# Memory-augmented attention mixed with a GEGLU: products of the memory from float16 pairs instead of float32

## The chip, the cores and the metric

The kernel runs on one core of a Trainium2 chip, as one launch. The metric is the device time of that launch in microseconds (us). Before the change it is 1577.5 us, the median of three runs (1577.44 to 1577.76). The inputs and the output are float32 in DRAM.

## What is computed

The input has 2048 tokens of D = 576 features. Its output is a mix, by a gate per token, of a segmented attention with a memory and of a feed-forward block with GELU gating:

```python
# attention, 32 heads of 18, four segments of 512 tokens
for s in range(4):
    qs, ks, vs = q[:, :, s], k[:, :, s], v[:, :, s]
    p = softmax(qs @ ks.T * 18**-0.5 + mask)         # within the segment
    a_dot = p @ vs
    pq = phi(qs)                                     # phi(t) = t + 1 if t > 0 else exp(t)
    a_mem = (pq @ M) / (pq @ z + 1e-6)
    o = g * a_mem + (1 - g) * a_dot                  # g = sigmoid(beta) per head
    pk = phi(ks)
    M = M + pk.T @ vs                                # 18 x 18 per head
    z = z + pk.sum(tokens)
a = concat(o) @ wo
b = (gelu(x @ w_gate) * (x @ w_up)) @ w_down         # 4608 hidden features
gate = sigmoid((x * gate_w).sum(-1))
out = gate * a + (1 - gate) * b
```

What the change touches is the line of M and the line of z. For each segment but the last, all heads' M and z are products over the segment's 512 tokens.

## The kernel before

**Float16 pairs.** For TensorE (PE) the kernel splits most operands into a high half (the value rounded to float16) and a low half (what is left, rounded to float16), and forms three products: high by high, high by low and low by high. The products of the memory are an exception: they are float32.

**The parts of the kernel.** The first part makes keys, queries and values, and the memory; it ends near 219 us of the profiled span. Then come 72 feed-forward steps (`step`, L1132), which hold the attention of all heads between their own products, and at the end the output projection. The change is in the first part, except that attention later reads the stored value pairs.

**The first part** has four stages s, one for each segment of 512 tokens. A stage first works on tokens in four quarters q of 128, and then on columns in nine groups j of 128 (queries and keys together have nine such groups). Stage 0 does its rows in a way of its own at the start (L623 to L684). From stage 1 on, with p = s - 1, the loop at L795 to L837 issues in each quarter:

- `vrows(s, q, 0)` (L518): the values of this quarter's tokens, heads 0 to 15, as fourteen float16 products of 288 columns into a PSUM bank.
- `put_rows` (L493): ScalarE (ACT) writes the high half of the value pairs to `vstage`, and for s up to 2 a float32 copy of the values to `v32`, whose last column in each head GpSimd (POOL) has set to 1. VectorE (DVE) writes the low half later (`rest`, L510), and then a DMA stores the pairs to DRAM for the attention.
- `key_rows(p, q - 1)` (L566): six float32 transposes of the previous segment's phi of keys (features by tokens, 128 x 512 tiles) to tokens by features; four go to a bank of the tag `st`, two to the bank `V`. ScalarE copies both to the tile `krow` in two pieces, of 448 and 192 columns.
- `beside_rows`, `behind_rows` (L706, L727): work of VectorE, ScalarE and GpSimd for the later feed-forward part, put here by quarter and stage. `form_sums` (L352) is the one that the prediction speaks of: in stages 2 and 3 it holds VectorE for more than a microsecond at a time.
- `recall(p, q)` (L534), from stage 2 on: phi of the queries of segment p times the memory as it stands, five float32 products into two banks of `st`; `put_recall` (L544) then divides by the z column on VectorE, which reads those banks until its end.
- `vrows(s, q, 1)` and `put_rows`: the same for heads 16 to 31 and two more columns (one is the mix's gate).
- `memorize(p, q - 1)` (L578): for each of the five spans of 128 features one float32 product, `krow` (as the stationary operand) by `v32` of the heads that the span touches, summed over the quarters in the banks `U` (spans 0 to 2) and `pv` (spans 3 and 4). A span touches 8 heads of 18 + 1 = 19 columns, so 152 columns; the last one, of 64 features, touches 4 heads, 76 columns. What a span has beside the heads' own blocks is masked away later.

Quarter 3's `key_rows` stands behind the loop over quarters, and its `memorize` behind the first column group.

Then, for each j, `project(s, j)` (L460) issues fourteen float16 products of 512 columns, and `put_columns` (L467), one group later, takes them out of PSUM: ScalarE writes the high half of queries and keys to `stage`, and the exponential part of phi; VectorE writes the linear part of phi (L480), its sum with the other (L481, or GpSimd) and the low half (`words`, L486), and a DMA stores the pairs. At j = 1, `keep_memory(p)` (L588) multiplies the products by the mask `bdm` and adds them to the block-diagonal memory `bd`, which the next recalls read. `make_gate` (L601) also stands there, and `beside_products` (L738) places side work by j.

**What sets the order.** For PE, ACT, DVE and POOL the order of the instructions on each engine is the order in which the program issues them (`manual_schedule(engines=ORDERED)`, L608). DVE's halves of `put_rows`, `put_columns` and `recall` are not issued where they are written: they are appended to the list `later`, and `finish_later` (L456) issues all of it, at two places in a quarter and one in a column group. The DMA queue (SP) is ordered by the framework. The pieces of one engine's queue are strictly in order, so an instruction that waits holds all behind it.

**Banks.** The program has eight PSUM banks of 512 float32 columns, given out by tag: `G`, `U`, `V` and `pv` have one each, `st` and `dn` two each, used in turn. A product into a bank waits until the bank's last reader is done. `project` uses `G` for j = 0, 4 and 8, `U` for 3 and 7, and `st` for the others.

## Time and profile before

One execution was profiled; that execution's span and engine totals are these:

| what | before |
|---|---|
| median of three runs | 1577.5 us |
| span of the profiled execution | 1576.7 us |
| instructions | 32594 |
| TensorE busy (matmul) | 1571.1 us, 100% |
| TensorE busy (weight loads, beside the matmuls) | 936.6 us, 59% |
| VectorE busy | 1134.6 us, 72% |
| ScalarE busy | 1175.1 us, 75% |
| GpSimd busy | 1209.5 us, 77% |
| DMA | 209.87 MB, 133 GB/s in the mean |

How to read what follows. Lines such as L585 are lines of the kernel before. PE is TensorE's matmul, PEld its weight load (the stationary operand), which runs beside the matmul ahead of it; DVE is VectorE, ACT ScalarE, POOL GpSimd. A timeline row gives the start, the length, the engine, the line, the operation, and output and input by the program's names with their shapes; "x12" joins twelve records that follow each other, and what stands in brackets is idle time ahead of it with what ended it. Matmul records of neighbours overlap, so that TensorE's pace is read from one start to the next, and a few matmul records are missing from a trace. The "chain that ended last" is followed back from the last instruction, at each step to what released it; its shares say which engine's work made up the span.

### The profile page before, as it was taken

The page shows a single profiled execution, that of the slowest core. Times are in us where ns is not written, and L with a number is a line of the kernel's source. Part 1 is how long each engine was busy: PE and PEld are TensorE (multiplying, and loading weights), DVE is VectorE, ACT ScalarE, POOL GpSimd, SP SyncE. Part 2 cuts the span into 40 slices and gives each one's busy share as a digit, 9 for nine tenths or more (in the row PEclk, how much of TensorE's full clock was granted, in tenths as well). Part 3 has the DMA queues.
Part 4 walks back from the last instruction along what each step waited for, and adds up shares of the span by engine and source line. Part 5 has one row for each costly group of instructions (what it writes and reads, how often), then busy time and mean ns, then how long its engine had stood idle before and what let it go on. Part 6 is the DMA issues. An engine that isn't in the chain of part 4 may idle for free.

```text
span 1576.7 us, 32594 instructions
## 1 busy us (share of the span) xinstructions
PE 1571.1 (100%) x11864; PEld 936.6 (59%) x11864; DVE 1134.6 (72%) x2974; ACT 1175.1 (75%) x1996; POOL 1209.5 (77%) x1173
## 2 busy tenths in 40 slices
PE   9999999999999999999999999999999999999999
PEld 6666754555555555555555555555555555555577
DVE  6667784777777777777777777777777777776665
ACT  6666454888888888888888888888888888886421
POOL 2233756788888888898988888887879797788697
PEclk9999999999999999999999999999999999999999
DMA  6532442587878798879787899888897887774644
GB/s 239 203 121 90 138 139 76 104 130 128 132 130 141 126 140 137 138 124 141 129 133 130 137 129 142 133 132 149 134 139 130 141 130 138 130 128 89 136 101 140
DMA packets 472680, 209.87 MB, mean 133 GB/s; under 512 B 427672, under 2 KB 437400, under 8 KB 472008
## 3 DMA queue, kind: packets, MB, share of 16 engines
q1 hardware_dynamic: 472520, 207.80, 71.3%
q8 instruction: 93, 1.52, 0.4%
q14 instruction: 67, 0.55, 0.1%
HBM read 91.87 MB, written 27.26 MB: 76 GB/s over the span
## 4 chain that ended last, share of the span: by engine, by line
PE 97%; DMA 1%; DVE 1%; ACT 1%; issue 0%; SPq 0%; DVEq 0%; ACTq 0%
PE dn L1007 27%; PE U L1047 18%; PE V L1047 12%; PE G L1047 12%; PE pv L962 4%; PE st L322 2%; PE U L1054 2%; PE G L322 2%; PE dn L332 2%; PE V L1059 1%; PE G L1059 1%; PE st L915 1%; PE U L322 1%; PE st L1367 1%; PE V L1054 1%; PE G L1054 1%
## 5 line engine op out<-in xcount | busy, mean ns | idle before, releaser
L942 POOL TENSOR_TENSOR ph<-pf,ph 128x512 f16<-128x512 f32 (+1 forms) x256 | 353.7, 1403 | 173.2 <-ACT ph L941 173.2
L1007 PE MATMUL dn<-paird,hh 128*128 128x288 f16 x3396 | 476.4, 286 | 0.0
L1047 PEld LDWEIGHTS <-pairg 128*128 128x128 f16 x3024 | 285.4, 98 | 304.4 <-issue 18.3
L1007 PEld LDWEIGHTS <-hh 128*128 128x128 f16 x3456 | 332.1, 98 | 153.4 <-issue 18.0
L1015 DVE SCALAR_TENSOR_TENSOR acc<-dn,ev,acc 128x288 f32<-128x288 f32 x534 | 274.3, 515 | 54.1 <-PE dn L1007 43.9
L931 ACT ACTIVATE pf<-pf,mb,esc 128x512 f32<-128x512 f32 (+3 forms) x512 | 292.9, 642 | 7.0 <-POOL ph L942 0.4
L1047 PE MATMUL G<-x,pairg 128*128 128x512 f16 x864 | 209.9, 379 | 0.2 <-DVE gl L1029 0.2
L1047 PE MATMUL U<-xt,pairg 128*128 128x512 f16 x864 | 210.0, 379 | 0.0
L1034 POOL TENSOR_TENSOR hh<-gl,hh 128x512 f16<-128x512 f32 x144 | 164.4, 1162 | 18.4 <-ACT hh L1033 18.4
L303 POOL TENSOR_TENSOR pairg<-raw,pairg 128x640 f16<-128x640 f32 (+2 forms) x144 | 174.2, 1232 | 5.1 <-ACT pairg L299 5.1
L299 ACT ACTIVATE pairg<-raw 128x640 f16<-128x640 f32 (+2 forms) x144 | 89.9, 650 | 112.9 <-POOL raw L293 65.1
L941 ACT ACTIVATE ph<-pf 128x512 f16<-128x512 f32 (+1 forms) x256 | 172.4, 720 | 0.0
L1192 DVE COPY gl<-U 128x512 f32<-128x512 f32 x72 | 49.8, 692 | 167.1 <-POOL hh L1034 150.1
L918 DVE CUSTOM_DVE_ANT_0 pf<-st,mask 128x512 f32<-128x512 f32 (+1 forms) x256 | 157.1, 614 | 0.0
L268 POOL TENSOR_SCALAR raw<-raw,sc 128x640 f32<-128x640 f32 x72 | 135.8, 1900 | 0.0
L918 DVE CUSTOM_DVE_ANT_0 pf<-dn,mask 128x256 f32<-128x256 f32 (+1 forms) x192 | 67.1, 375 | 81.6 <-PE dn L915 81.2
L1037 ACT ACTIVATE gl<-gl,sc 128x512 f32<-128x512 f32 x144 | 96.6, 715 | 37.1 <-DVE gl L1218 19.3
L1047 PE MATMUL V<-xt,pairg 128*128 128x512 f16 x432 | 105.7, 381 | 0.0
L1047 PE MATMUL U<-x,pairg 128*128 128x512 f16 x432 | 105.0, 379 | 0.0
L1047 PE MATMUL V<-x,pairg 128*128 128x512 f16 x432 | 104.8, 378 | 0.0
L1033 ACT ACTIVATE hh<-gl 128x512 f16<-128x512 f32 x144 | 82.6, 616 | 16.6 <-DVE gl L1029 16.5
L962 PEld LDWEIGHTS <-pt 128*128 128x128 f16 x2560 | 83.4, 96 | 6.3
(305 smaller groups left out, 2641.1 us busy)
## 6 DMA issues: line engine op xcount, KB each, us to landing
raw<-in_wgu_dram SPq DMA_DIRECT2D x36, 640.0 KB
rawd<-in_wd_dram SPq DMA_DIRECT2D x36, 288.0 KB
qt<-qk SPq DMA_DIRECT2D x132, 72.0 KB
kt<-qk SPq DMA_DIRECT2D x132, 72.0 KB
qk<-stage SPq DMA_DIRECT2D x36, 256.0 KB
qt<-qk SPq DMA_DIRECT2D x132, 36.0 KB
kt<-qk SPq DMA_DIRECT2D x132, 36.0 KB
vp<-vstage SPq DMA_DIRECT2D x16, 296.0 KB
```

Source lines behind the costliest of these rows:

```text
L268: pool.tensor_scalar(r, r, scl[f // 2][0][:, 0:1], None, OP.mult)
L303: pool.tensor_tensor(spot(f, *p, 1), raw_g[f][:, p[0] : p[1]], spot(f, *p, 0), OP.subtract)
L918: dve.tensor_tensor_reduce(prob[a][:, COL[qi] : COL[qi + 1]], out[qi], mask[:, L - (qi + 1) * P :], 1.0, -3e38, OP.add, OP.max, mx[a][:, q ...
L931: act.activation(r, r, AF.Exp, bias=b[:, qi : qi + 1], scale=esc[:, 0, c : c + 1])
L941: act.activation(h[:, 0, cols], p[:, cols], AF.Copy)
L942: pool.tensor_tensor(h[:, 1, cols], p[:, cols], h[:, 0, cols], OP.subtract)
L962: pe.matmul(ov, pr[:, 10 * i + COL[qi] // P + kb], v[:, 4 * e + kb, c0 : c0 + VC], start=kb == 0 and i == 0, stop=kb == qi and i == 1)
L1007: pe.matmul(o[:, :NH], hh[:, a, q * P : (q + 1) * P], w[:, b, n * NH : (n + 1) * NH], start=i == 0, stop=i == 5)
L1015: dve.scalar_tensor_tensor(av, o[:, :NH], ev, av, OP.mult, OP.add)
L1034: pool.tensor_tensor(hh[:, 1], t, hh[:, 0], OP.subtract)
L1037: act.activation(t, o, AF.Gelu_apprx_tanh, scale=scl[f // 2][0][:, 2 + c : 3 + c])
L1047: pe.matmul(o, w[:, i, (a + k) * P : (a + k + 1) * P], x[:, b + k], start=start and k == 0 and i == 0 and b == h, stop=k == 1 and i == 1, ...
```

## The change

The products of the memory are made of float16 pairs, in `memorize`, as three products for each span: high keys by high values with the ones column (19 columns a head), high keys by low values (18), and low keys by high values with the ones column (19). All three are summed in the same bank.

- **Values.** The float32 copy `v32` and its memset are gone. `memorize` reads the pairs that are stored for the attention anyway, `vstage`, straight from SBUF. For this, a head's 37 columns are stored as [low, high, 1] instead of [high, low, 1], so that the high half and the 1 lie side by side. A product's moving operand then has runs of 18 or 19 elements, 37 apart. `vstage` gets six buffers instead of four.
- **Keys.** `krow` is now a pair of float16 tiles. ScalarE writes the high half as it takes the transposed keys out of PSUM, times a power of two; VectorE writes the low half from the same PSUM banks (`low`, two instructions, appended to `later`).
- **Scales.** The pairs need the keys within float16's range. `key_scale(p)` works out the power of two in four one-column instructions on VectorE, in quarter 0 of the next stage, and `memory_scale(p)` in three more, ahead of `project(s, 0)`, the factors that undo it. `keep_memory` first scales the z columns (two instructions more) and applies the other factor with the mask in one instruction (`scalar_tensor_tensor` for `tensor_tensor`).
- **Banks.** From stage 1 on, the first four transposes of the keys go to `G` instead of `st`, and `project(s, 0)` to `dn` instead of `G`.
- **Order.** `recall(p, q)` now stands behind the second `vrows` of its quarter instead of ahead of it, and so directly ahead of `memorize`. `memorize(p, 3)` is preceded by a `finish_later()`.

```diff
--- before.py
+++ after.py
@@ -393,2 +393,3 @@
     esc = cst.tile([P, 2, 4], F32, name="esc")
+    kmc = cst.tile([P, 3, 4], F32, name="kmc")
     gha = cst.tile([P, 4, H], F32, name="gha")
@@ -409,3 +410,3 @@
         pa = first.enter_context(tc.tile_pool(name="early", bufs=2, reuse_waits="tile"))
-        W, phi, vst, v32, kr, mem = {}, {}, {}, {}, {}, {}
+        W, phi, vst, kr, mem = {}, {}, {}, {}, {}
         QG = ((0, 1), (2, 3), (4, 5), (6, 7), (8,))
@@ -427,3 +428,3 @@
             if on_act:
-                junk = pa.tile([P, KT * P], F32, name="krow", bufs=2).bitcast(BF16)
+                junk = flat(pa.tile([P, 2, KT * P], F16, name="krow", bufs=2)).bitcast(BF16)
                 act.activation(junk[:, : r.shape[1]], r, AF.Square, accum_out=o)
@@ -462,3 +463,3 @@
             i = j % 4
-            pr = bank("G") if i == 0 else bank("U") if i == 3 else bank("st", 2)
+            pr = bank("dn", 2) if s and j == 0 else bank("G") if i == 0 else bank("U") if i == 3 else bank("st", 2)
             chain_w(pr, lambda k, a: w[:, a, k * P : (k + 1) * P], x16[s])
@@ -497,7 +498,4 @@
             if b == 0:
-                st = vst[s, q] = pa.tile([P, H, VC], F16, name="vstage", bufs=4)
+                st = vst[s, q] = pa.tile([P, H, VC], F16, name="vstage", bufs=6)
                 pool.memset(st[:, :, VC - 1 : VC], 1.0)
-                if s <= 2:
-                    v32[s, q] = pa.tile([P, H, MC], F32, name="v32", bufs=6)
-                    pool.memset(v32[s, q][:, :, DH:], 1.0)
             st = vst[s, q]
@@ -505,8 +503,6 @@
             hs = slice(16 * b, 16 * b + 16)
-            act.activation(st[:, hs, 0:DH], p3, AF.Copy, scale=unit)
-            if s <= 2:
-                act.activation(v32[s, q][:, hs, 0:DH], p3, AF.Copy, scale=a)
+            act.activation(st[:, hs, DH : 2 * DH], p3, AF.Copy, scale=unit)

             def rest():
-                dve.scalar_tensor_tensor(st[:, hs, DH : 2 * DH], p3, unit, st[:, hs, 0:DH], OP.mult, OP.subtract)
+                dve.scalar_tensor_tensor(st[:, hs, 0:DH], p3, unit, st[:, hs, DH : 2 * DH], OP.mult, OP.subtract)
                 if b:
@@ -566,3 +562,3 @@
         def key_rows(s, q):
-            ka, kb = bank("st", 2), bank("V")
+            ka, kb = bank("G") if s else bank("st", 2), bank("V")
             tok = slice(q * P, (q + 1) * P)
@@ -573,5 +569,12 @@
                 pe.transpose(kb[:, i * P : (i + 1) * P], phi[s, j][:, tok], ident)
-            k = kr[s, q] = pa.tile([P, KT * P], F32, name="krow", bufs=2)
-            act.activation(k[:, :448], ka[:, 64:], AF.Copy)
-            act.activation(k[:, 448:], kb[:, :192], AF.Copy)
+            k = kr[s, q] = pa.tile([P, 2, KT * P], F16, name="krow", bufs=2)
+            sc = kmc[:, s, 1:2]
+            for o, r in ((slice(0, 448), ka[:, 64:]), (slice(448, KT * P), kb[:, :192])):
+                act.activation(k[:, 0, o], r, AF.Copy, scale=sc)
+
+            def low():
+                for o, r in ((slice(0, 448), ka[:, 64:]), (slice(448, KT * P), kb[:, :192])):
+                    dve.scalar_tensor_tensor(k[:, 1, o], r, sc, k[:, 0, o], OP.mult, OP.subtract)
+
+            later.append(low)

@@ -580,3 +583,3 @@
                 mem[s] = bank("U"), bank("pv")
-            k, v = kr.pop((s, q)), v32.pop((s, q))
+            k, v = kr.pop((s, q)), vst.pop((s, q))
             for j, (a, w) in enumerate(SPANS):
@@ -584,4 +587,7 @@
                 o = mem[s][j // 3][:, (j % 3) * 8 * MC : (j % 3) * 8 * MC + (h1 - h0) * MC]
-                pe.matmul(o, k[:, a : a + P], v[:, h0:h1].rearrange("p h d -> p (h d)"),
-                          start=q == 0 and j % 3 == 0, stop=q == 3 and j in (2, 4), skip_group_check=True)
+                o = o.rearrange("p (h d) -> p h d", d=MC)
+                for i, c in ((0, slice(DH, VC)), (0, slice(0, DH)), (1, slice(DH, VC))):
+                    pe.matmul(o[:, :, : c.stop - c.start], k[:, i, a : a + P], v[:, h0:h1, c],
+                              start=q == 0 and j % 3 == 0 and i == 0 and c.start == DH,
+                              stop=q == 3 and j in (2, 4) and i == 1, skip_group_check=True)

@@ -590,2 +596,6 @@
             n = 8 * MC
+            sm, zf = kmc[:, s, 2:3], kmc[:, s, 3:4]
+            for o, h in ((ka, 24), (kb, 12)):
+                z = o[:, : h * MC].rearrange("p (h d) -> p h d", d=MC)[:, :, DH:]
+                dve.tensor_scalar(z, z, zf, None, OP.mult)
             for o, d, k in ((ka[:, : 3 * n], flat(bd[:, 0:3]), flat(bdm[:, 0:3])),
@@ -594,7 +604,20 @@
                 if s == 0:
-                    dve.tensor_tensor(d, o, k, OP.mult)
+                    dve.scalar_tensor_tensor(d, o, sm[: o.shape[0]], k, OP.mult, OP.mult)
                 else:
-                    m = pa.tile([P, KT * P], F32, name="krow", bufs=2)[: o.shape[0], : o.shape[1]]
-                    dve.tensor_tensor(m, o, k, OP.mult)
+                    m = flat(pa.tile([P, 2, KT * P], F16, name="krow", bufs=2)).bitcast(F32)[: o.shape[0], : o.shape[1]]
+                    dve.scalar_tensor_tensor(m, o, sm[: o.shape[0]], k, OP.mult, OP.mult)
                     dve.tensor_tensor(d, d, m, OP.add)
+
+        def key_scale(s):
+            fl, iv, sm, zf = (kmc[:, s, i : i + 1] for i in range(4))
+            dve.tensor_scalar(sm, al[:, s, 0:1], 2.0**30, 1.0, OP.mult, OP.add)
+            dve.tensor_scalar(fl.bitcast(I32), sm.bitcast(I32), EXP, None, OP.bitwise_and)
+            dve.tensor_scalar(iv.bitcast(I32), fl.bitcast(I32), EXP, None, OP.bitwise_xor)
+            dve.tensor_scalar(iv, iv, 2.0**13, None, OP.mult)
+
+        def memory_scale(s):
+            fl, iv, sm, zf = (kmc[:, s, i : i + 1] for i in range(4))
+            dve.tensor_scalar(sm, fl, al[:, s, 1:2], None, OP.mult)
+            dve.tensor_scalar(zf.bitcast(I32), al[:, s, 1:2].bitcast(I32), EXP, None, OP.bitwise_xor)
+            dve.tensor_scalar(zf, zf, 2.0**-15, None, OP.mult)

@@ -805,2 +828,4 @@
                             key_rows(p, q - 1)
+                        else:
+                            key_scale(p)
                         beside_rows(s, q)
@@ -810,6 +835,6 @@
                         behind_rows(s, q)
+                        pv = vrows(s, q, 1)
+                        put_rows(s, q, 1, *pv)
                         if p >= 1:
                             recall(p, q)
-                        pv = vrows(s, q, 1)
-                        put_rows(s, q, 1, *pv)
                         if q:
@@ -821,4 +846,7 @@
                         make_gate(s)
+                    if s and j == 0:
+                        memory_scale(p)
                     pr = project(s, j)
                     if s and j == 0:
+                        finish_later()
                         memorize(p, 3)
```

## The prediction

> **What bounds the kernel now.** I read the page first (span, engines, granted clock, the chain that ended last), then the busy time of TensorE in the three stretches in which memory's products stand, then the timeline there.
>
> ```profile
> span 1576.7 us, 32594 instructions
> ...
> PE 1571.1 (100%) x11864; PEld 936.6 (59%) x11864; DVE 1134.6 (72%) x2974; ACT 1175.1 (75%) x1996; POOL 1209.5 (77%) x1173
> ...
> PEclk9999999999999999999999999999999999999999
> ...
> PE 97%; DMA 1%; DVE 1%; ACT 1%; issue 0%; SPq 0%; DVEq 0%; ACTq 0%
> ```
>
> TensorE is busy all the time at the full granted clock and holds 97% of the chain. The same for the stretches (columns: stretch, length, PE busy and records, clock, DMA share, GB/s):
>
> ```profile
> 61.67:75.22 13.55, 13.55 (x114) 1.00 0.24 90
> 111.72:129.90 18.18, 18.18 (x149) 1.00 0.26 100
> 166.99:185.09 18.10, 18.10 (x150) 1.00 0.27 102
> ```
>
> So a microsecond of TensorE's stream taken out or put in there is a microsecond of the kernel, as long as no product has to wait for VectorE or ScalarE. A record's length is not its cost: records overlap, and the cost is the distance from one start to the next. What the change takes from ScalarE (the v32 copies) and GpSimd (its memsets) I count at nothing, since TensorE covers it.
>
> **1. Memory's products.** Float32 now, ten records a call (120 in all, so 12 calls):
>
> ```profile
> L585 PE MATMUL U<-v,krow x72: 290/292/293, 63.4 to 189.4; 128*128 128x152 f32 x72
> L585 PE MATMUL pv<-v,krow x48: 227/282/294, 64.2 to 189.9; 128*128 128x152 f32 x24, 128*128 128x76 f32 x24
> ```
>
> ```profile
> 63.39 0.94 PE L585 MATMUL U<-v,krow 128*128 128x152 f32 x6
> ...
> 68.70 0.94 PE L585 MATMUL U<-v,krow 128*128 128x152 f32 x6
> ...
> 69.91 1.63 PE L332 MATMUL dn<-wv,x 128*128 128x288 f16 x12
> 71.38 0.29 PE L334 MATMUL dn<-wv,x 128*128 128x288 f16 x1
> ```
>
> A call lasts from 68.70 to 69.91, 1.21 us. The new one issues fifteen float16 products: four spans of 152 + 144 + 152 columns and one of 76 + 72 + 76, 2016 columns. The float16 stream behind it gives the price: 12 products of 288 columns from 69.91 to 71.38, 122.5 ns each or 0.425 ns a column. That makes 0.86 us a call, 0.35 us less; twelve calls: **-4.2 us**.
>
> This holds only if a product's pace is its columns. The new ones are smaller than 288, each with its own weight load, and the moving operand lies in runs of 18 or 19 elements with gaps. No row shows that operand; the ends are set by these:
>
> ```profile
> 607.31 0.66 PE L962 MATMUL pv<-vt,pt 128*128 128x37 f16 x20
> 607.90 0.39 PE L1059 MATMUL G<-x,pairg 64*128 64x512 f16 x1
> ```
>
> ```profile
> L962 PEld LDWEIGHTS <-pt 128*128 128x128 f16 x2560 | 83.4, 96 | 6.3
> ```
>
> Twenty products of 37 columns, each with a 128x128 float16 load, start within 0.59 us: 30 ns each, under the 64 ns that 152 columns need, so loads hide. The other end is a pace of the load's own record, 96 ns: 15 x 96 = 1.44 us a call, 0.23 more than now, +2.8 us. Half the column rate from the gaps would give 1.72 us, +6.1 us. Below 0.86 us it can't go, as the columns must pass. I take 0.86: the 37-column row is the nearest in kind. Every ns of pace is worth 15 x 12 = 0.18 us; at 81 ns nothing is gained.
>
> The Trainium skill (page "TensorE: Matmul & The Clock Gate", section "Back-to-back issue gap") says that a stream of load and matmul pairs is spaced about 81 ns at 128 columns, and about 131 ns at 512. By an estimate from that page the new call would last 1.2 us and the gain would vanish. The rows above disagree at both ends: 30 ns at 37 columns, and 122.5 ns already at 288.
>
> **2. Waits that go.** With another bank for transposed keys, recall no longer shares `st` with them. In stage 2 its second half waits, in quarters 1 to 3, until ScalarE has copied the keys out of the bank it is to take:
>
> ```profile
> 107.07 1.37 PE L540 MATMUL st<-bd,phi 128*128 128x152 f32 x10
> ...
> 112.38 1.54 PE L540 MATMUL st<-bd,phi 128*128 128x152 f32 x10
> ...
> 119.06 1.54 PE L540 MATMUL st<-bd,phi 128*128 128x152 f32 x10
> ...
> 125.75 1.54 PE L540 MATMUL st<-bd,phi 128*128 128x152 f32 x10
> ```
>
> Three times 0.17: -0.5 us. In stage 3 the first transposes wait for put_recall's last reading of `st`:
>
> ```profile
> 166.44 0.29 PE L335 MATMUL U<-wv,x 128*128 128x288 f16 x1
> 166.99 0.63 PE L571 MATMUL st<-ident,phi 128*128 128x128 f32 x4 [0.26 <-DVE mo L562]
> ```
>
> 0.55 us from start to start in place of 0.12: -0.4 us. G, the new bank, was last read by the held words of column group 8, a quarter before. For project(s, 0) the `dn` buffer is that of quarter 3's first rows, long evacuated.
>
> **3. The wait that comes.** Each call's third product now needs the low half of the keys, which VectorE writes last in its queue: behind put_recall, the sums for the feed-forward products, the rows' rests, and then the two new subtractions. Their length is not in the trace; one over 288 columns takes 0.46, one over 512 0.68 (rows below), so 0.61 for the first (448) and 0.37 for the second (192), which only the eleventh and twelfth products need.
>
> *Stage 1, quarter 1* is late already: the chain starts at a `stage` buffer that a DMA frees late.
>
> ```profile
> 59.69 0.75 DVE L480 TENSOR_SCALAR phi<-G,al 128x512 f32<-128x512 f32 x1 [1.56 <-ACT expm L475]
> 60.55 0.69 DVE L481 TENSOR_TENSOR phi<-phi,expm 128x512 f32<-128x512 f32 x1
> 61.16 0.45 DVE L511 SCALAR_TENSOR_TENSOR vstage<-dn,vstage 128x288 f16<-128x288 f32 x1
> 61.53 0.68 DVE L486 SCALAR_TENSOR_TENSOR stage<-G,stage 128x512 f16<-128x512 f32 x1
> 62.12 0.45 DVE L511 SCALAR_TENSOR_TENSOR vstage<-dn,vstage 128x288 f16<-128x288 f32 x1
> 62.49 0.21 DVE L513 TENSOR_SCALAR gate<-dn,al 128x1 f32<-128x1 f32 x1
> 62.62 0.45 DVE L511 SCALAR_TENSOR_TENSOR vstage<-U,vstage 128x288 f16<-128x288 f32 x1
> ```
>
> Between 61.16 and the first L511 go key_scale's four dependent one-column operations. Such ones stand 0.19 us apart here, even while GpSimd works:
>
> ```profile
> 231.66 3.75 POOL L268 TENSOR_SCALAR raw<-raw,sc 128x640 f32<-128x640 f32 x2
> ...
> 233.80 0.15 DVE L98 TENSOR_SCALAR wz<-zo 128x1 f32<-128x1 f32 x1
> ...
> 233.99 0.15 DVE L77 TENSOR_SCALAR va<-wz 128x1 int32<-128x1 int32 x1
> ```
>
> Three distances and an end, 0.64 us: 61.80. Then the paces of the rows above, 0.37 + 0.59 + 0.37 + 0.13 + 0.37: 63.63, and the first low half until 64.24. The third product would have started 0.13 us behind 63.39, at 63.52; with about 0.15 for the hand-over and the weight load it starts at 64.4: **+0.9 us** (0.5 to 1.2, by the unknown length and the four operations). What queues behind it is all of TensorE.
>
> *Other quarters.* In stage 1, quarters 2 and 3, the keys' copies start right behind the transposes, so the low half is there some 1.3 us behind them, and 1.7 us of rows' products stand in between: nothing. In stage 2 the round of VectorE is the question:
>
> ```profile
> 113.95 0.18 DVE L551 COPY mo<-st 128x19 f32<-128x19 f32 x1 [0.66 <-PE st L540]
> ...
> 115.29 0.82 DVE L562 TENSOR_TENSOR mo<-st,rden 128x396 f32<-128x396 f32 x2
> ...
> 117.02 1.27 DVE L364 SCALAR_TENSOR_TENSOR xt<-acc,xsc,xt 128x1024 f16<-128x1024 f32 x1
> ...
> 119.44 0.46 DVE L511 SCALAR_TENSOR_TENSOR vstage<-dn,vstage 128x288 f16<-128x288 f32 x1
> ```
>
> ```profile
> 116.69 1.63 PE L332 MATMUL dn<-wv,x 128*128 128x288 f16 x12
> ...
> 123.38 1.63 PE L332 MATMUL dn<-wv,x 128*128 128x288 f16 x12
> ```
>
> From recall's end to the end of the first low half: 0.2 + put_recall 2.1 (113.95 to 116.1) + the two sums 2.42 (117.02 to 119.44) + 0.37 + 0.61 = 5.7 us. TensorE's quarter is 6.69 now (116.69 to 123.38), 6.17 with the terms above, and recall now stands right ahead of memory's products, so the third product comes 6.2 us behind recall's end: 0.5 us to spare. But all of VectorE's round, with the second low half and the other rest, sums to some 6.2 too, so little more fits. In stage 3 the sums stand behind the low half; only quarter 1, where VectorE first waits for ScalarE's squares, comes within about 0.2 us. The calls for quarter 3 have a projection of 3 us as cover. I count all these at nothing; they are the first to go wrong.
>
> *keep_memory* gets two small scalings, 0.3 us of VectorE, where the bank it frees is needed two projections later: nothing. SP's queue has a load of wgu ahead of the first two wd loads at stage 3's end, which are needed some 20 us later: nothing. From the attention steps on each engine's order is as before.
>
> **Sum:** -4.2 - 0.5 - 0.4 + 0.9 = -4.2 us: a span of 1572.5. The median shown, 1577.5, lies 0.8 us over the profiled span; the same 4.2 off gives **1573.3 us**. About 0.2%, 3.2 us, is what a measurement of this kernel can tell from no change, so the forecast clears that by one microsecond only.
>
> **The rivals.**
>
> A: the low half is late elsewhere too. For it: VectorE's full round in stage 2, and quarter 1 of stage 3. Against it: 0.5 us to spare where most calls stand. If the two subtractions took 0.6 us more together, stage 1 would lose 0.8, stage 2 0.7 and stage 3 0.4 more: 1575.2; with more GpSimd interference, up to 1577. Chance 0.18, mostly within 0.2%.
>
> B: small pairs run at a pace near 81 ns, and part 1's term is nothing: 1577.5 (what goes and what comes in the waits cancel). For it: the load's 96 ns record. Against it: 30 ns at 37 columns. 0.06. The page named above is the rule that says so.
>
> C: the start of the feed-forward steps doesn't move, since VectorE, whose queue is nearly without a gap in stage 3's projections, hands over at its own time: about 1577. Its work there follows TensorE's, however. 0.06.
>
> D, slower: the moving operand's gaps halve the column rate in all 180 products. The call lasts 1.72 us, +0.51 x 12 = +6.1 in place of -4.2: 1583.6. It decides from a factor of 1.4, where the gain is gone, and from about 1.7 it is slower beyond 0.2%. For it: no row has such an operand. Against it: nothing seen. 0.08.
>
> **How the numbers follow.** Forecast 0.62, A 0.18 (a fifth of it still faster), B 0.06, C 0.06, D 0.08. Faster 0.62 + 0.04 = 0.66; within 0.2% 0.14 + 0.06 + 0.06 = 0.26; slower 0.08. The range takes in the forecast's own bounds (1572.0 with no new wait and 0.3 to spare, 1574) and A, B and C, and leaves out D: 1572.0 to 1577.8.
>
> **What would show it.** The feed-forward steps begin here:
>
> ```profile
> 219.04 1.46 PE L1047 MATMUL V<-xt,pairg 128*128 128x512 f16 x6
> ```
>
> The new products' starts 64 ns apart at 152 columns, 0.86 us a call (1.2 for B, 1.7 for D). Recall at 1.37 in every quarter of stage 2, and no wait ahead of stage 3's first transposes. One gap of about 0.9 us ahead of the third product of the first call, and none over 0.2 ahead of the eleven others; gaps in stages 2 and 3 are A. First feed-forward product some 4 us earlier than this; if it is earlier but the span isn't shorter by as much, C.

## The result and the profile after

The changed kernel takes 1575.49 us (median of 21 runs, 1574.54 to 1576.65) against 1577.52 us before (21 runs, 1577.00 to 1578.65). The ratio is 0.9986, with a 95% interval of 0.998 to 0.9992: faster by 2.0 us. The forecast was 4.2.

The page of the changed kernel answers to the page of the kernel before:

```profile
span 1574.5 us, 32715 instructions
...
PE 1568.0 (100%) x11924; PEld 932.9 (59%) x11924; DVE 1148.0 (73%) x3025; ACT 1169.5 (74%) x1972; POOL 1209.7 (77%) x1161
```

The span is 2.2 us shorter and still full of TensorE. VectorE has 13.4 us more to do, ScalarE 5.6 less. Medians lie 0.8 to 2.7 us above the span of the one profiled execution, kernel by kernel, where a run's time lies 1.7 to 2.2 us above its own span; the two executions compared here are both about 1 us slower than their kernel's median. So a trace says where time goes, and the medians say how much when a few tenths are in question.

**Where the 2 us are.** Four places of TensorE's stream add up to the difference.

*A call of memorize* (timeline of TensorE, the changed kernel, stage 1, second call; L590 is the new product's line):

```profile
69.55 0.81 PE L590 MATMUL U<-vstage,krow 128*128 128x152 f16 x9
70.19 0.48 PE L590 MATMUL pv<-vstage,krow 128*128 128x152 f16 x6
70.51 1.63 PE L332 MATMUL dn<-wv,x 128*128 128x288 f16 x12
```

From the first start to the next line's start, 69.55 to 70.51, it lasts 0.96 us, not 1.21 as before and not 0.86 as forecast: -0.25 x 12 = -3.0 us. By their starts, 152 columns take 71 to 73.5 ns (medians of each of the fifteen places in a call), 144 take 68 to 70.

*Recall and transposes in stages 2 and 3* don't wait any more. The rows of stage 2, quarter 1:

```profile
111.73 0.29 PE L335 MATMUL U<-wv,x 128*128 128x288 f16 x1
111.85 0.60 PE L567 MATMUL G<-ident,phi 128*128 128x128 f32 x4
...
114.24 1.37 PE L536 MATMUL st<-bd,phi 128*128 128x152 f32 x10
115.45 0.81 PE L590 MATMUL U<-vstage,krow 128*128 128x152 f16 x9
```

The transposes start 0.12 us behind the rows' last product, and recall lasts 1.37 where it lasted 1.54 in three quarters. That is -0.9 us with stage 3's transposes, as forecast.

*Stage 1, quarter 1* lost more. TensorE before and then after:

```profile
58.91 1.63 PE L332 MATMUL U<-wv,x 128*128 128x288 f16 x12
...
60.63 0.60 PE L571 MATMUL st<-ident,phi 128*128 128x128 f32 x4
61.30 0.44 PE L573 MATMUL V<-ident,phi 128*128 128x128 f32 x2
61.67 1.64 PE L332 MATMUL dn<-wv,x 128*128 128x290 f16 x12
...
64.60 1.63 PE L332 MATMUL dn<-wv,x 128*128 128x288 f16 x12
```

```profile
58.61 1.63 PE L332 MATMUL U<-wv,x 128*128 128x288 f16 x12
...
60.32 0.60 PE L567 MATMUL st<-ident,phi 128*128 128x128 f32 x4
61.58 0.44 PE L569 MATMUL V<-ident,phi 128*128 128x128 f32 x2 [0.66 <-DVE kmc L613]
62.57 1.64 PE L332 MATMUL dn<-wv,x 128*128 128x290 f16 x12 [0.55 <-DVE vstage L507]
...
64.30 1.00 PE L590 MATMUL U<-vstage,krow 128*128 128x152 f16 x9
65.13 0.48 PE L590 MATMUL pv<-vstage,krow 128*128 128x152 f16 x6
65.45 1.63 PE L332 MATMUL dn<-wv,x 128*128 128x288 f16 x12
```

From the rows into U to the end of the call it was 5.69 us, and is 6.84. With the call's own 0.25 taken off, new waiting is 1.4 us. Only 0.2 of it stands inside the call (the nine products into U take 0.83 us here, 0.64 in the second call). The rest is ahead of the fifth transpose and ahead of the second rows. Before this place TensorE is 0.3 us earlier than it was (58.61 against 58.91), which I had not counted, and which it waits away here. This execution is a late one: in the traces of experiments 1, 4, 6, 7, 8 and 12, whose kernels have the same order up to this call, it is 4.9 to 5.4 us from the rows into U to the call, and not 5.69.

*The start of the feed-forward steps* gives 0.7 us back:

```profile
216.25 1.46 PE L1075 MATMUL V<-xt,pairg 128*128 128x512 f16 x6
217.71 1.46 PE L1075 MATMUL G<-x,pairg 128*128 128x512 f16 x6
219.52 1.46 PE L1075 MATMUL V<-x,pairg 128*128 128x512 f16 x6 [0.36 <-DVE gl L1143]
...
222.68 1.46 PE L1075 MATMUL G<-x,pairg 128*128 128x512 f16 x6
```

The first product stands 2.8 us earlier than the 219.04 of before (-3.0 - 0.9 + 1.4 - 0.3). The product at 222.68 stood at 224.79 in the kernel before, and is only 2.1 us earlier. From there on the two streams keep their distance within 0.3 us to the end.

### The profile page after: what moved, and what is told of

It reads as the page before. It is cut to its first block, busy times and chain, and to the rows that moved or that the text cites. A ratio compares the mean times of both kernels' runs of the same rounds, so it can differ in the third digit from the quotient of the medians.

```text
span 1574.5 us, 32715 instructions
## 1 busy us (share of the span) xinstructions
PE 1568.0 (100%) x11924; PEld 932.9 (59%) x11924; DVE 1148.0 (73%) x3025; ACT 1169.5 (74%) x1972; POOL 1209.7 (77%) x1161
## 3 DMA queue, kind: packets, MB, share of 16 engines
q8 instruction: 94, 1.54, 0.4%
## 4 chain that ended last, share of the span: by engine, by line
PE 95%; DVE 2%; ACT 1%; POOL 1%; issue 1%; DMA 1%; SPq 0%; POOLq 0%; DVEq 0%
PE dn L1035 27%; PE U L1075 18%; PE V L1075 12%; PE G L1075 12%; PE pv L990 4%; PE U L1082 2%; PE dn L332 2%; PE st L322 1%; PE G L1087 1%; PE V L1087 1%; PE st L943 1%; PE st L1395 1%; PE G L1082 1%; PE V L1082 1%; PE dn L943 1%; PE G L322 1%
## 5 line engine op out<-in xcount | busy, mean ns | idle before, releaser
L299 ACT ACTIVATE pairg<-raw 128x640 f16<-128x640 f32 (+2 forms) x144 | 90.0, 650 | 114.3 <-POOL raw L293 66.3
```

## The experiments

My theory after the result: about 1 of the missing 2.2 us is waits that have nothing to do with TensorE's own work, and the rest is the price of a small product with a broken moving operand. Each kernel below is compared with the kernel before on its own chip; the ratio is to that, with its 95% interval.

**1. An unbroken moving operand** (label e1_contiguous)

```diff
-                    pe.matmul(o[:, :, : c.stop - c.start], k[:, i, a : a + P], v[:, h0:h1, c],
+                    pe.matmul(o[:, :, : c.stop - c.start], k[:, i, a : a + P],
+                              flat(v)[:, h0 * VC + c.start :][:, : (h1 - h0) * (c.stop - c.start)],
```

> The changed kernel, but each product of the memory reads as many columns as before from one unbroken run of the value pairs, instead of eight runs of 19 or 18 (so the memory's values are not the reference's). In the changed kernel 152 columns take 72 ns from start to start, 144 take 69, a call 0.96 us. Theory (the runs cost): 152 columns take about 65 ns, a call 0.86 us, and the products are 1.2 us shorter in all; of this 0.8 to 1.0 us reach the span, since VectorE, which has no gap from 179 us on, holds back what the last calls gain: 0.8 us below the changed kernel. Rival (a product this small costs 6 to 9 ns beside its columns, by its weight load or by its bank): 72 ns stay, and the time is that of the changed kernel within 0.3 us.

1574.76 us, ratio 0.9982 (0.9974 to 0.9991): 0.7 us below the changed kernel. Its second call (timeline of TensorE):

```profile
69.01 0.76 PE L590 MATMUL U<-vstage,krow 128*128 128x152 f16 x9
69.61 0.47 PE L590 MATMUL pv<-vstage,krow 128*128 128x152 f16 x6
69.91 1.27 PE L332 MATMUL dn<-wv,x 128*128 128x288 f16 x9
```

The call lasts 0.90 us; 144 columns take 61.5 to 65 ns instead of 68 to 70, and 152 take 65 to 74 instead of 71 to 73.5. So the runs of 18 and 19 elements cost 0.06 us a call, 0.7 us in all. The other 0.05 us over the forecast's 0.86 stay with products of this size, and why is open. The Trainium skill (page "Advanced Engine Details and Errata", section "Memory Cachelines") says that an SBUF access to a new 16-byte line each time pays a penalty, and that any gap in PSUM slows matmuls significantly. In size the trace agrees only in part: gaps in the moving operand cost 0.06 us of a call's 0.96 (a run here is 36 or 38 bytes long, so that most accesses stay in a line), and products that leave out every nineteenth column of their PSUM output (the 144 columns, here too) run at 61.5 to 65 ns, near the pace of their columns.

**2. key_scale a stage sooner** (e2_scale_early)

```diff
-                        else:
-                            key_scale(p)
...
                     if j == 1:
                         make_gate(s)
+                        if s < 3:
+                            key_scale(s)
```

> The changed kernel with key_scale's four instructions at column group 1 of the stage ahead, not in quarter 0 of the next one. Theory (these four stand ahead of the rests that free a bank for the second rows of stage 1, quarter 1): the second rows' first product there comes about 0.6 us earlier than now (0.55 us of idle time goes), the first call's third product waits 0.1 to 0.2 us as now, and the time is 0.6 us below the changed kernel. Rival (ScalarE's late start behind the stage buffer sets this place, whatever VectorE does): under 0.2 us.

1574.46 us, ratio 0.9981 (0.9972 to 0.9990): 1.0 us below the changed kernel, more than the 0.6 expected. Both waits ahead of the first call are gone in its trace, not only the one at the second rows. The rows of VectorE in the changed kernel show what was taken away:

```profile
60.83 0.69 DVE L482 TENSOR_TENSOR phi<-phi,expm 128x512 f32<-128x512 f32 x1
61.44 0.15 DVE L613 TENSOR_SCALAR kmc<-al 128x1 f32<-128x1 f32 x1
...
61.99 0.15 DVE L616 TENSOR_SCALAR kmc<-kmc 128x1 f32<-128x1 f32 x1
62.07 0.45 DVE L507 SCALAR_TENSOR_TENSOR vstage<-dn,vstage 128x288 f16<-128x288 f32 x1
...
63.88 0.68 DVE L577 SCALAR_TENSOR_TENSOR krow<-st,kmc,krow 128x448 f16<-128x448 f32 x1
```

The four instructions take 0.63 us (61.44 to 62.07) ahead of the L507 that frees the bank for the second rows. That explains 0.6. In the traces the chain also starts sooner, which is not this edit's doing: its start lies in ScalarE (evacuation of column group 8; before, after, and this experiment):

```profile
58.49 0.60 ACT L470 ACTIVATE stage<-G 128x512 f16<-128x512 f32 x1 [3.78 <-DMA qk<-stage]
```

```profile
58.77 0.60 ACT L471 ACTIVATE stage<-G 128x512 f16<-128x512 f32 x1 [2.60 <-PE dn L335]
```

```profile
57.61 0.60 ACT L471 ACTIVATE stage<-G 128x512 f16<-128x512 f32 x1 [3.47 <-DMA qk<-stage]
```

ScalarE's order is the same in the last two, and the instruction starts at 58.77 in one execution and at 57.61 in the other; it waits for a DMA that frees a buffer of `stage`. In the six kernels that are alike up to there (experiments 1, 4, 6, 7, 8 and 12) it starts at 58.0 to 58.3. (In the changed kernel's row the trace names a product instead; experiment 5 shows that it was the buffer.) With an earlier landing there is slack, and the wait for the fifth transpose goes with it. Whether that makes the other 0.4 us of the medians is not shown, as single runs of each of the two kernels lie 1.8 and 2.1 us apart.

**3. The banks alone, on the kernel before** (e3_banks_alone)

```diff
-            pr = bank("G") if i == 0 else ...
+            pr = bank("dn", 2) if s and j == 0 else bank("G") if i == 0 else ...
...
-            ka, kb = bank("st", 2), bank("V")
+            ka, kb = bank("G") if s else bank("st", 2), bank("V")
```

> The kernel before with the two changes of banks alone (keys to G from stage 1 on, project(s, 0) to dn); products in float32, order as before. Theory (the bank waits of stages 2 and 3, three of 0.17 us and one of 0.42, go and reach the end): 0.9 us below the kernel before. Rival (VectorE's queue at the end of stage 3 holds it back): under 0.3 us.

1576.73 us, ratio 0.9994 (0.9985 to 1.0002): 1.0 us below the kernel before by the medians, near the expected 0.9, but the interval takes in no change. In its trace the waits for `st` are gone: the transposes of stage 3 start 0.12 us behind the rows, and recall in stage 2 takes the same time in all four quarters.

**4. The old banks in the changed kernel** (e4_old_banks): the same two lines the other way round.

> The changed kernel with the banks of before (keys to st, project(s, 0) to G), all else as changed. Theory (the banks are worth 0.9 us, and st is held longer now, because VectorE reads the keys there too): recall and the transposes wait for st in stages 2 and 3, 0.9 to 3 us above the changed kernel, about the time of before or over it. Rival (the new place of recall behind the second rows already keeps it from meeting the keys): the changed kernel's time within 0.3 us.

1581.28 us, ratio 1.0025 (1.0016 to 1.0034): slower than the kernel before. Its table of TensorE's waits from 50 us on (line, what it waited for, total, times, longest):

```profile
PE st L567 <- DVE mo L558: 5.2, 4, 1.8
```

The transposes wait for put_recall's last reading of `st`, four times, up to 1.8 us. In the kernel before that wait happened once, for 0.4 us. Which of two things did it, VectorE's longer round or recall's later place, this kernel can't tell; experiment 12 does. Beside the new products the bank change is worth 5.8 us, not the 0.9 that it is worth by itself.

**5. Four buffers of stage** (e8_four_stages)

```diff
-            st = pp.tile([P, 2, L], F16, name="stage", bufs=3)
+            st = pp.tile([P, 2, L], F16, name="stage", bufs=4)
```

> The changed kernel with four buffers of stage instead of three. In all profiles so far ScalarE's evacuation of column group 8 in stage 0 waits until 57.6 to 58.8 us for a DMA that frees a stage buffer, 1 to 2 us after ScalarE has nothing else to do, and stage 1's quarter 1 follows from there. Theory (this transfer, with key_scale's 0.6 us on top, makes the 1.2 us of idle time ahead of the first call, and its landing differs from run to run): the evacuation starts near 56.5 us, both waits of TensorE there go, 1.0 to 1.4 us below the changed kernel, and runs differ less. Rival (key_scale alone makes it): 0.3 us or less.

1574.36 us, ratio 0.9979 (0.9970 to 0.9988): 1.1 us below the changed kernel, as expected. ScalarE and TensorE of this kernel:

```profile
54.49 0.60 ACT L471 ACTIVATE stage<-G 128x512 f16<-128x512 f32 x1 [0.77 <-PE G L325]
```

```profile
58.09 1.63 PE L332 MATMUL U<-wv,x 128*128 128x288 f16 x12
...
60.24 0.38 PE L569 MATMUL V<-ident,phi 128*128 128x128 f32 x2
60.46 1.64 PE L332 MATMUL dn<-wv,x 128*128 128x290 f16 x12
...
62.19 0.80 PE L590 MATMUL U<-vstage,krow 128*128 128x152 f16 x9
```

The evacuation starts right behind its product, 4 us sooner, and both waits of TensorE and the one inside the call are gone with key_scale where it was. From the rows into U to the call it is 4.1 us instead of 5.7. So the missing buffer starts the wait, and key_scale's 0.6 us came on top only because of it.

**6. Recall ahead of the second rows again** (e5_recall_ahead)

```diff
+                        if p >= 1:
+                            recall(p, q)
                         pv = vrows(s, q, 1)
                         put_rows(s, q, 1, *pv)
-                        if p >= 1:
-                            recall(p, q)
```

> The changed kernel with recall back ahead of its quarter's second rows; banks and products as changed. Theory (in the changed kernel VectorE's last reading of st ends 0.7 to 1.0 us ahead of where recall would then stand, so the new order isn't needed for st once the keys are in G, and VectorE's round is full either way): within 0.4 us of the changed kernel. Rival (recall meets put_recall's reading of st in stages 2 and 3): waits of TensorE on mo, 0.5 to 2 us above the changed kernel.

1575.22 us, ratio 0.9986 (0.9977 to 0.9995): the changed kernel's time within 0.3 us, and no new wait. The move of recall is worth nothing by itself here.

**7. Two sums of squares sooner** (e6_squares_sooner)

```diff
                     if j == 7:
                         ...
+                        squares(1, 3, 1, act_square)
+                        squares(1, 1, 2, act_square)
                     if j == 8:
                         high_g(1, 1)
                         low_g(1, 1)
-                        squares(1, 3, 1, act_square)
-                        squares(1, 1, 2, act_square)
```

> The changed kernel with two of ScalarE's sums of squares (0.9 us each) at column group 7 of stage 3 instead of 8, where ScalarE stands idle for 1.1 us twice; they no longer stand ahead of its last evacuation of G. Theory (at the start of the feed-forward steps TensorE waits for a chain of ScalarE's evacuation of G, VectorE's low half and put_recall, and that is why 0.6 to 0.7 us of what the first part gains are lost there): the evacuation of G starts about 1 us sooner after its product, the 0.36 us of idle time at V goes, and the time is 0.5 us below the changed kernel. Rival (VectorE's own queue, full since 179 us, is late by as much): under 0.2 us, the wait on V stays.

1574.26 us, ratio 0.9978 (0.9969 to 0.9987): 1.2 us below the changed kernel, 0.5 expected. ScalarE at the end of stage 3, the changed kernel and then this one:

```profile
212.63 1.26 ACT L299 ACTIVATE pairg<-raw 128x640 f16<-128x640 f32 x2 [1.07 <-POOL raw L293]
213.79 0.72 ACT L86 ACTIVATE junk<-raw 128x640 bf16<-128x640 f32 x1
...
216.36 0.58 ACT L471 ACTIVATE stage<-G 128x512 f16<-128x512 f32 x1
```

```profile
214.78 0.60 ACT L471 ACTIVATE stage<-G 128x512 f16<-128x512 f32 x1 [0.30 <-PE G L325]
```

And what TensorE does there in this kernel:

```profile
215.79 1.46 PE L1075 MATMUL V<-xt,pairg 128*128 128x512 f16 x6
217.08 1.46 PE L1075 MATMUL G<-x,pairg 128*128 128x512 f16 x6
218.38 1.46 PE L1075 MATMUL V<-x,pairg 128*128 128x512 f16 x6
```

The evacuation follows its product, and the three groups stand 1.30 us apart, without a wait: 0.7 us of TensorE. The other 0.5 us are not explained. The two profiled executions differ by another 0.46 us, by which the first call of stage 1 begins sooner here, at a place that the edit doesn't touch; that says how much executions differ, and nothing of the medians.

**8. No low halves of the keys** (e7_no_low)

```diff
-            later.append(low)
...
-                    pe.matmul(o[:, :, : c.stop - c.start], k[:, i, a : a + P], v[:, h0:h1, c],
+                    pe.matmul(o[:, :, : c.stop - c.start], k[:, 0, a : a + P], v[:, h0:h1, c],
```

> The changed kernel without the low halves of the keys: VectorE's two subtractions a call are left out, and the third product of each span reads the high keys again (the products count high keys twice). TensorE's work is as in the changed kernel. Theory (VectorE's 12.6 us more are what makes it late at the start of the feed-forward steps, and the third product of the first call waits 0.2 us for them): the wait at V goes, 0.7 us below the changed kernel. Rival (VectorE has room, ScalarE and GpSimd set that place): 0.2 us below, the wait at V stays.

1574.56 us, ratio 0.9981 (0.9972 to 0.9990): 0.9 us below the changed kernel. The wait on V at the feed-forward steps is gone, as theory had it, though ScalarE's order is the changed kernel's. So that place has two parents: VectorE's 13 us more, and ScalarE's two sums ahead of the last evacuation; taking away either is enough. They meet by way of GpSimd: ahead of the two sums stands L299, which waits 1.07 us for GpSimd in the changed kernel (first row of experiment 7) and not at all here. How GpSimd, which adds up the parts of phi that VectorE and ScalarE make, came to be late was not followed link by link.

**9. The sums sooner in the kernel before** (e11_before_squares): the edit of experiment 7 on the kernel before.

> The kernel before with the two sums of squares at column group 7 alone. Theory (in the kernel before VectorE arrives at the feed-forward steps just in time, with 0.2 us of waiting, and only the change's earlier TensorE and 12.6 us more of VectorE make it late): 0.2 us below the kernel before, not told from it. Rival (a gain that was there all along and has nothing to do with the change): 0.7 to 1.2 us below, as in the changed kernel.

1577.98 us, ratio 1.0001 (0.9992 to 1.0009): nothing. VectorE's busy time in the stretch from 179 to 216 us, of the kernel before and of the changed kernel, says why (columns: stretch, length, busy, clock, DMA share, GB/s):

```profile
179.00:216.00 37.00, 31.21 (x61) 1.00 0.35 122
```

```profile
179.00:216.00 37.00, 35.66 (x74) 1.00 0.37 129
```

Before, VectorE had 5.8 us of idle time there, and ScalarE's two sums ended in time for the last evacuation (218.03, right behind its product at 217.61). After, it has 1.3 us, and the late evacuation is passed on.

**10. The three repairs together** (e9_three_repairs: experiments 2, 5 and 7)

> The changed kernel with the three repairs together: key_scale's instructions a stage sooner, two sums of squares at column group 7, four buffers of stage. Theory (two waits give the change's gain back, that of stage 1, quarter 1, which four buffers alone already took away, and that at the start of the feed-forward steps): no wait of TensorE but the one on x at the start of stage 1; 1573.6 us, 0.7 below four buffers alone. Rival (what the first part gains is lost again later): 1574.3 us.

1573.79 us (1573.21 to 1574.03), ratio 0.9975 (0.9965 to 0.9985): 3.9 us below the kernel before and near the 1573.6 expected, and its 8 runs lie 0.8 us apart where the changed kernel's 21 lie 2.1 apart. TensorE's waits from 50 to 230 us, all that is left:

```profile
PE dn L334 <- DVE x L180: 0.2, 1, 0.2
```

**11. Unbroken runs, made by GpSimd** (e10_repairs_unbroken: experiment 10, and in `put_rows`)

```diff
+                    if s <= 2:
+                        for o, c in ((v16[s, q][:, : H * MC], slice(DH, VC)), (v16[s, q][:, H * MC :], slice(0, DH))):
+                            pool.tensor_copy(o.rearrange("p (h d) -> p h d", h=H), st[:, :, c])
```

> The three repairs together, and GpSimd copies each quarter's value pairs once more, to one unbroken run of high halves with ones and one of low halves, which the memory's products read (vstage has four buffers again). Nothing is left out. Theory (unbroken runs make a call 0.06 us shorter, and GpSimd, busy for 2 to 4 tenths there, has room): 0.7 us below the three repairs without it, 1573.0 us. Rival (GpSimd's copies hold up VectorE's instructions that touch SBUF alone, or come late): no gain, or 0.3 to 1 us above it.

The products then read `v16`. 1575.11 us, ratio 0.9983 (0.9974 to 0.9992): 1.3 us above experiment 10, the rival's outcome and more. A call does get shorter, to 0.90 us. But its waits of TensorE are these:

```profile
PE dn L334 <- DVE x L180: 1.3, 1, 1.3
PE U L595 <- DVE krow L582: 0.3, 1, 0.3
```

The wait for stage 1's tokens grows from 0.2 to 1.3 us, and a low half of the keys comes 0.3 late. The two add 1.4 us, and the shorter calls take off 0.8; by the medians the loss is larger, and the rest wasn't traced. That the copies in stage 0 delay the chain to L180 is likely, but was not followed link by link.

**12. The old banks and recall ahead** (e12_old_banks_order: experiments 4 and 6 together, so that the new products stand in the old banks and the old order)

> The changed kernel with the old banks and recall ahead of the second rows, as in the kernel before: the new products alone, with what they need of VectorE. The old banks alone cost 5.8 us, in four waits of the transposes for put_recall, 0.4 to 1.9 us each. Theory (recall's new place, 1.7 us later, makes these waits; with recall ahead VectorE is done with st 1.7 us sooner): the four waits fall under 0.3 us each, the time is 0.5 to 1.5 us above the changed kernel, and the new banks are worth 1 us and not 5.8. Rival (VectorE's longer round makes them, whatever the place of recall): 3 us or more above the changed kernel.

1580.87 us, ratio 1.0019 (1.0009 to 1.0028): 5.4 us above the changed kernel. My theory falls. The waits of the transposes do shrink to 0.3 us and less, as it said, but others take their place (TensorE's waits from 50 to 230 us):

```profile
PE st L536 <- DVE krow L577: 3.4, 6, 1.1
...
PE st L567 <- DVE mo L558: 0.5, 2, 0.3
```

Recall, six times, now waits for the second reader that the change gives to the keys' bank, VectorE's subtraction of the low half; in the kernel before it waited there for ScalarE's copy, three times 0.17 us. In both places of recall that were tried, a bank that it shares with the keys is held too long by VectorE. So the bank change is a condition of the new products, not an extra.

## Why the prediction was right in its sign and half wrong in its size

- **The forecast as a whole.** -4.2 us forecast, -2.0 measured. The measured time lies in the stated range, but the range also took in rivals A, B and C. By the prediction's own division the outcome, 0.14%, is "within 0.2%", to which it gave 0.26, and not the change beyond 0.2% to which it gave 0.66. The 0.2% itself was too wide a line: the interval of 21 runs each tells 0.14% from no change.
- **Part 1, the products: the mechanism right, the term mis-sized.** -4.2 forecast, -3.0 measured. The step that failed is "if a product's pace is its columns": 0.425 ns a column from products of 288 columns, where 152 take 72 ns (0.474). It had bounds for gaps and loads (up to 96 ns) and took the optimistic end, because the 37-column row hides its load. That row shows 30 ns for 37 columns, which is 0.8 ns a column: it was evidence of a cost beside the columns, and I read it only as a bound on loads. Of the 1.2 us missing here, 0.7 are the broken runs (experiment 1).
- **Part 2, the waits that go: right**, -0.9 forecast, and so in the traces. But the change of banks was priced as an extra, and experiments 4 and 12 show that without it the kernel is 3.2 to 3.6 us slower than before. The text asked what the new reader of the keys costs the product that waits for its result, and not what it costs the next user of the bank that it reads.
- **Part 3, the wait that comes: the chain right, its first hand-over to TensorE missed.** The sum had VectorE's chain from key_scale to the end of the first low half at 3.1 us (61.16 to 64.24) and the third product at 64.4. Measured are 3.1 us (61.44 to 64.56, without idle time between) and 64.6. What the text missed is the L507 inside that chain: it frees a bank for the second rows, so that most of the waiting stands ahead of them and only 0.2 us at the third product. The end of the chain decides all the same, so this adds nothing. The 1.4 us of waiting instead of 0.9 are 0.3 by which TensorE came sooner, and had to wait for the same chain, and 0.2 by which the third product came later than forecast (the chain began and ended 0.3 later, and the hand-over to TensorE took 0.1 less). In five other traces with the same order and the low halves (experiments 1, 4, 6, 7 and 12) the third product starts at 63.9 to 64.2, so that 64.6 is this execution's. The DMA that starts the chain was named as a fact of one execution, while ScalarE's start behind it differs by 0.8 us between executions of kernels alike up to there.
- **Other quarters: right.** No gap over 0.2 us in the eleven other calls; rival A is out. The places that it named as tight are so; the first low halves there (stage 2, quarter 3, and stage 3, quarter 1):

```profile
126.93 0.68 DVE L577 SCALAR_TENSOR_TENSOR krow<-G,kmc,krow 128x448 f16<-128x448 f32 x1
```

```profile
168.27 0.67 DVE L577 SCALAR_TENSOR_TENSOR krow<-G,kmc,krow 128x448 f16<-128x448 f32 x1
```

They end at 127.61 and 168.94, and the third products start at 128.13 and 169.12: 0.5 and 0.2 us to spare, as forecast.
- **Rival B:** out. 72 ns at 152 columns, each with a load of its own, are less than the 81 at which nothing is gained. The rule of the Trainium skill (page "TensorE: Matmul & The Clock Gate", section "Back-to-back issue gap"), about 81 ns at 128 columns and 131 at 512, does not hold here: the six products of 512 columns in the rows of experiment 7 take 1.30 us, 217 ns each. **Rival D:** a factor of 1.1, far from the 1.4 at which it would decide.
- **Rival C, given 0.06, came true in part.** It was set aside because VectorE's "work there follows TensorE's". Before, it did; but the change itself gives VectorE 13 us more, and the sum never added that to VectorE's own queue up to stage 3's end, nor asked who waits for VectorE there. 0.7 us were lost (experiments 7 to 9).
- **Not in the sum:** 0.3 us that TensorE gains ahead of stage 1, and loses in stage 1's wait. In the seven traces with this order the place lies between 58.46 and 58.84, in the three with the order before between 58.74 and 58.91, so that in the mean it is 0.2.

Together: 1.2 us from the products, 0.2 from stage 1 (0.5 of waiting less the 0.3) and 0.7 from the feed-forward start is the 2.1 us between forecast and result, as far as one execution of each kernel says. With the repairs the change gives 3.9 us, near the forecast only by chance: the products still miss 1.2, the wait of 0.9 is gone, and about 0.4 us come from stage 1, quarter 1, where the kernel before waited too (61.30 and 61.67 above are 0.23 and 0.15 us later than the rows of experiment 5 space them). The four buffers were not tried on the kernel before, so that these 0.4 us are read from its trace alone.

## What to carry to other kernels

When work moves from TensorE to VectorE, add it to VectorE's own round, stretch by stretch, up to the next hand-over, and ask which banks it now reads and who takes them next; the free time that covered it may be spent before the gain reaches the end. Price a small product by a row of its own size and layout, and where none exists, not by the pace of a large one alone: a line through the two sizes on record here, 30 ns at 37 columns and 122.5 at 288, gives 0.99 us a call as a second bound beside 0.86, and 0.96 was measured. A wait at a buffer that a DMA frees differs between executions; a fourth buffer takes it away at its start, and by the medians gained as much (1.1 us) as reordering behind it (1.0 us), but not more.

## What the runs showed of the hardware that I had not expected

A float16 product of 152 columns in eight runs of 19 takes 71 to 73.5 ns from start to start, and 65 to 74 in one run; 144 columns take 68 to 70 in runs of 18, and 61.5 to 65 in one run. A gap of one column in nineteen in the PSUM output cost nothing that shows. The landing of one and the same DMA store moved ScalarE's next instruction between 58.0 and 58.8 us from execution to execution of kernels that are alike up to there, and a fourth buffer brought it to 54.5.
